# Projections with 128-row operands, the second feed-forward layer of two blocks by seven products, and a new instruction order

## The chip, the cores and the metric

One Trainium2 chip; the program runs on one of its NeuronCores. Five engines work side by side: PE (matrix multiply, with its weight loads listed as PEld), DVE (vector), ACT (activation), POOL (GpSimd) and SP, which here only issues DMAs. The metric is the device time of one execution in microseconds (us), the median over repeated executions.

## The reference

For 8 batches x 8 heads, 576 tokens, head size 64 and 128 random features, a linear attention is computed, and its output (4608 tokens x 512) goes through two dense layers of width 2048.

```python
def phi(x):                                  # x scaled by 64 ** -0.25
    proj = einsum('bhsd,md->bhsm', x, omega) # 64 -> 128
    h = proj - sum(x * x, -1) / 2
    return exp(h - max(h, -1)) / sqrt(m)
kv, z = einsum('bhsm,bhsd->bhmd', k_p, v), sum(k_p, 2)
num, den = einsum('bhsm,bhmd->bhsd', q_p, kv), einsum('bhsm,bhm->bhs', q_p, z) + 1e-6
h = x @ w_in                                 # x = num / den, 4608 x 512; w_in 512 x 2048
out = maximum(0.01 * h, h) @ w_out           # w_out 2048 x 512
```

All of it is float32; `q` is drawn 4.679 times as wide as `k` and `v`.

## The kernel before, in words

**Numbers in two halves.** A float32 operand of a matmul is scaled by a power of two and split into two float16 halves, high and low. A product takes three matmuls: high x high, high x low, low x high. Every split is an instruction on ACT or DVE that rounds (`high`, L331 on ACT) and one on DVE or POOL that subtracts (`low_`, L337).

**Feed-forward.** The 4608 tokens are 9 blocks of 512 (`feed_forward(j)`, j = 0 to 8). The first layer of blocks 0 and 1 is done plainly (L967). From block 2 on (`FIRST_FAST`) it is done by Strassen's method in Winograd's form: both matrices are cut into 2 x 2 quarters and 7 products of quarters take the place of 8 (`fast_first_layer`, L1007). The 2048 features are cut into four quads `q`; each quad has 7 products of 12 matmuls with 256 columns, whose weights come from a DRAM copy `w1d`. The intermediate results are copied out of PSUM (`so_far`, L331), added (`add`, L1023), passed through the leaky ReLU (L1030) and split into halves in the four tiles `big`. The second layer of every block is plain: four groups of 128 tokens, 48 matmuls of 512 columns each (`down`, L1084), 192 per block, one scaled copy out of PSUM and one store per group.

**Attention.** `Unit` prepares 512 (or 640) tokens of one pair of heads: load, squares and their sums, a scale, the two halves of the scaled tokens side by side in `z` (L539 to L562), and a transposing DMA `t<-z`. `project` (L578) then multiplies by omega. The two heads of a pair lie in the upper and the lower 64 rows, so every matmul uses 64 rows and there are three for each head and tile of 128 tokens: 24 for a unit of four tiles, 6 for the extra fifth tile of a key unit. Key batches 0 and 1 and query block 0 take another form in float32 (`Whole`, L645). Features then go through maximum, exponential and splitting; the sums over keys are at L773 to L775, the query products at L852 to L854.

**Order.** The kernel records all operations with a cost per engine and the tiles that they read and write; `Plan.order` then lays out one list of instructions per engine from these costs, priorities (`prio`), paces (`PACE`, `LATER`) and slacks (`SLACK`). Feed-forward matmuls are fillers: they go where PE has nothing more urgent. At run time each engine works its list strictly in that order.

**Start.** Before the feed-forward can run, w_in must be read as int64 words and rebuilt (L453 to L476), its scale found (sums over PE at L466, L486) and split (L500); and query block 0 must have passed through attention, up to the division at L872, the halves `xn` and the transposing DMA `xt<-xn`.

Of the kernel before, what the change touches and what calls it, by code (L numbers as in the profile page):

```python
# [30 lines left out]
SIGN_POOL = {"w1": [0, 1, 3, 4, 5, 7], "w2": [0, 1, 3, 7]}  # L31
SPLIT_DVE = {"w1": [0, 1, 2, 4, 5, 7], "w2": [0, 1, 2, 3, 4, 5]}
Z_POOL = {"k": 4, "q": 3}
PACE = {"k": 17.0506, "q": 9.805, "w1": 0, "w1s": 3.6719, "w2": 15.9561, "w2s": 15.0}

WHOLE = 2
FIRST_FAST = 2
OPS = ("A11", "A12", "A22", "S1", "S2", "S3", "S4")
SLOT = {"B11": 0, "B21": 1, "B22": 2, "B12": 3, "T1": 4, "T3": 5, "T2": 6, "T4": 7}
SLACK = {"PE": 0.5, "chain": 0.093}  # L40
SUMS_DVE = []
LATER = {"w1": -37.7982, "w2": 35.2434, "k": -22.3577, "q": -876.3298, "f": 0.0319, "s": -0.056}
# [5 lines left out]
OUT_UP = 2.0 ** 15 * 2.0 ** (-14 * 3)  # L48
# [19 lines left out]
class Plan:  # L68
# [7 lines left out]
    def __init__(self, places):  # L76
        self.places, self.ops, self.over = places, [], {}
        self.wrote, self.read, self.kinds = {}, {}, {}
        self.now, self.nth = (None, 0.0), 0
# [10 lines left out]
    def op(self, ways, r=(), w=(), prio=0.0, slack=0.0, moved=0):  # L90
# [4 lines left out]
        o.ways, o.prio, o.slack, o.moved = {e: way for e, *way in ways}, prio, slack, moved  # L95
        name, pace, self.nth = self.now[0], self.now[1], self.nth + 1
# [20 lines left out]
    def order(self):  # L117
# [51 lines left out]
        while len(done) < len(self.ops):  # L169
# [4 lines left out]
            for o in sorted(open_, key=lambda o: (o.prio, o.number)):  # L174
# [3 lines left out]
                if filler:  # L178
                    t += SLACK["PE"] * o.slack
# [24 lines left out]
            end = t + o.cost  # L204
# [3 lines left out]
            if e == "SP":  # L208
                ports = max(ports, end) + o.moved / 400e3
                end = ports + 1.9  # L210
            else:
                end += self.HOP[e]
# [43 lines left out]
def performer_ffn(ctx: ExitStack, tc, qT, kT, qn, kn, vn, omT, eye, w_in, w_out, out):  # L256
# [53 lines left out]
    for i in (6, 7):  # L310
        over["xt", len(tiles["xt"])] = [("w1", i)]
        tiles["xt"].append(tiles["w1"][i].bitcast(F16).rearrange("p (i c d) -> p i c d", i=2, c=8))
    plan = Plan({k: len(v) for k, v in tiles.items()})
# [49 lines left out]
    def power_of_two(mx, name, prio, one_=ONE):  # L363
# [6 lines left out]
           r=[f"mx_{name}", "ident"], w=["scratch"], prio=prio, slack=1.0)  # L370
# [46 lines left out]
    class Weight:  # L417
# [26 lines left out]
        def convert(self, i, prio):  # L444
# [17 lines left out]
            def sums():  # L462
# [6 lines left out]
               slack=6.0)  # L469
# [9 lines left out]
        def scale(self, prio):  # L479
# [11 lines left out]
            self.pow, self.key = power_of_two(mx, self.name, prio, ONE / 4 if self.name == "w1" else ONE)  # L491
# [28 lines left out]
    class Unit:  # L520


        def __init__(self, what, i, hp, prio):
            self.what, self.i, self.hp, self.prio = what, i, hp, prio
            tiles_ = key_tiles(i) if what == "k" else range(4 * i, 4 * i + 4)
            self.t0, self.nt = tiles_[0] * P, len(tiles_)

        def prepare(self):
# [15 lines left out]
            def scales():  # L544
# [6 lines left out]
                nc.vector.tensor_scalar(sc[:, 3:4], sc[:, 1:2], om_c, None, op0=ALU.mult)  # L551
            op("DVE", 0.65, scales, r=[self.sq, "om_c"], w=[self.sc], prio=prio)
            heads = lambda: at(nat)[:, :nt, :]
            up = lambda: at(self.sc)[:, 2:3]
            zh, zl = (lambda i=i: at(z)[:, :2 * nt, :].rearrange("p (c i) x -> p c i x", i=2)[:, :, i] for i in range(2))
# [11 lines left out]
        def features(self, c0, nc_, ph, part):  # L567
# [13 lines left out]
            op("PE", 3 * nc_ * 0.057, project, r=[self.t, "om"], w=[pj], prio=prio, slack=1.0)  # L581
# [6 lines left out]

            def bias():
                nc.vector.scalar_tensor_tensor(rows(1), rows(0), down(), sq(), op0=ALU.mult, op1=ALU.subtract)  # L590
# [3 lines left out]
            op("DVE", dve(n * M), lambda: nc.vector.scalar_tensor_tensor(p(), pv(), down(),  # L594
               row(2).rearrange("p (g o) -> p g o", o=1).broadcast_to([P, n, M]), op0=ALU.mult, op1=ALU.add),
               r=[pj, st, self.sc], w=[p32], prio=prio)
            op("ACT", act(n * M, 1), lambda: nc.scalar.activation(flat(p()), flat(p()), AF.Exp, bias=shift), w=[p32],  # L597
               r=["ones"], prio=prio)
# [12 lines left out]
    class Whole:  # L611
# [21 lines left out]
        def features(self, c0, nt, p32, p):  # L633
# [5 lines left out]
            def project():  # L639
# [9 lines left out]
               slack=1.0)  # L649
# [82 lines left out]
    def key_batch(b, prio):  # L732

        values(b, prio)
# [4 lines left out]
        for hp in range(HP):  # L739
            plan.like("k", PACE["k"])  # L740
            if b >= WHOLE:
# [12 lines left out]
            if b < WHOLE:  # L754
                def sums(u=u, edge=edge, acc=acc, hp=hp, parts=parts):
# [7 lines left out]
                   slack=1.0)  # L763
            else:
                def sums(u=u, edge=edge, acc=acc, hp=hp, parts=parts):
# [11 lines left out]
                   *((v, x) for x in (0, 1, 2, 3)), (v, "ones", 0), (v, "ones", 1)], w=[acc], prio=prio, slack=1.0)  # L777
# [19 lines left out]
    def parted(j, xn, xt, at_, n, src, keys, prio):  # L797
# [5 lines left out]
        low_(n * P, lambda: part(1), x, lambda: part(0), r=[*keys, (xn, 0)], engines=("POOL", "DVE"), w=[(xn, 1)],  # L803
             prio=prio)
# [3 lines left out]
    def query_block(j, prio):  # L808

        for hp in range(HP):  # L810
            plan.like("q", PACE["q"])
            u = Unit("q", j, hp, prio) if j else Whole("q", j, hp, prio)
# [25 lines left out]
            for i in range(2):  # L838
# [22 lines left out]
                if j:  # L861
                    op("PE", 12 * 0.031, num, r=[(qp, 0), (qp, 1), *((kvs[b], hp | 1) for b in used)], w=[acc],
                       prio=prio, slack=1.0)
# [48 lines left out]
    def fast_weights():  # L912
# [8 lines left out]
        for u in range(4):  # L921
            for k in range(2):
                b, b2 = buf("wt"), buf("wt")
                t = lambda i, b=b: at(b)[:, 256 * i:256 * i + 256]
# [22 lines left out]

    def feed_forward(j):
        plan.like()
        top, work = -1.0, 1e6 + j  # L950
        gs = [buf("big") for _ in range(4)]
        fast = j >= FIRST_FAST
# [28 lines left out]

        def fast_first_layer():
# [8 lines left out]
            def four_tiles(q):  # L991
                pair = lambda b: at(b).rearrange("p (f t) -> p f t", f=2)
# [186 lines left out]
```

## Time and profile before

| | us |
|---|---|
| median of 3 runs | 962.62 (961.75 to 963.24) |
| the profiled execution | 963.96 |
| its span, first to last instruction | 962.2 |
| PE busy in the span | 903.2 (94%) |
| DVE, ACT, POOL busy | 668.5, 574.1, 349.2 |
[...]

The profile shows one execution. Busy time of an engine is the time in which at least one of its instructions ran. In the timeline's rows of PE the duration of a group includes the run-out of its last matmul, so two groups that follow each other overlap on paper; the distance from one start to the next is what a group costs.

### The profile page before, as it was taken

What the parts mean: (1) busy time and instruction counts of PE and PEld (TensorE: products, weight loads), DVE (VectorE), ACT (ScalarE), POOL (GpSimd) and SP (SyncE); (2) the same over time, 40 slices, a digit from 0 to 9 for tenths busy, and PEclk for the clock granted to TensorE, in tenths of its full rate; (3) what the DMA queues carried; (4) which work ended last, traced back from release to release, by engine and by line L of the source; (5) the groups of instructions that cost most, each with busy time, mean ns of one, the idle gap of its engine ahead of it and who ended that gap; (6) DMA issues with size and microseconds to landing.
All of it is one profiled execution on the core that took longest, in us unless ns stands there. A gap on an engine that the chain in (4) does not pass through costs nothing.

```text
span 962.2 us, 20553 instructions
## 1 busy us (share of the span) xinstructions
PE 903.2 (94%) x8286; PEld 596.3 (62%) x8286; DVE 668.5 (69%) x1236; ACT 574.1 (60%) x833; POOL 349.2 (36%) x318
## 2 busy tenths in 40 slices
PE   4886999999998889999999999999999999999998
PEld 4785466445454775578557855785587558746843
DVE  7988998787689598878888787768788862200200
ACT  5686796647756676468746854686477634603520
POOL 2323346566755661116212621251125223400510
PEclk7778899999999999999999999999999999999999
DMA  9687335957398999799879878997689785623300
GB/s 369 264 238 244 67 56 116 223 155 176 59 195 210 296 277 209 166 238 239 185 179 234 203 195 184 221 238 158 140 217 236 149 149 160 172 57 102 96 12 33
DMA packets 278080, 171.19 MB, mean 178 GB/s; under 512 B 195296, under 2 KB 240096, under 8 KB 276960
## 3 DMA queue, kind: packets, MB, share of 16 engines
q1 hardware_dynamic: 277984, 169.87, 71.7%
q8 instruction: 65, 1.06, 0.5%
q14 instruction: 31, 0.25, 0.1%
HBM read 105.87 MB, written 16.78 MB: 127 GB/s over the span
## 4 chain that ended last, share of the span: by engine, by line
PE 70%; DVE 7%; DMA 7%; ACT 3%; issue 1%; SPq 1%; POOL 0%; ACTq 0%; DVEq 0%
PE ffn L1084 20%; PE ffn L1007 12%; PE pj L1084 11%; PE pj L1007 10%; PE ffn L967 7%; PE pj L578 4%; DMA qp<-ph 3%; DMA t<-z 2%; DMA w<-w1d 1%; PE pj L967 1%; DVE p L594 1%; ACT row L331 1%; DVE ph L337 1%; PE mi L852 1%; DVE st L586 1%
## 5 line engine op out<-in xcount | busy, mean ns | idle before, releaser
L337 POOL TENSOR_TENSOR big<-row,big 128x512 f16<-128x512 f32 x144 | 181.0, 1271 | 306.0 <-ACT big L331 284.0
L1084 PEld LDWEIGHTS <-big 128*128 128x128 f16 x1728 | 163.3, 98 | 183.8 <-issue 0.8
L1007 PEld LDWEIGHTS <-w 128*128 128x128 f16 x2352 | 227.1, 98 | 43.2 <-issue 8.7
L1084 PE MATMUL ffn<-wt,big 128*128 128x512 f16 x1056 | 246.4, 379 | 0.0
L1084 PE MATMUL pj<-wt,big 128*128 128x512 f16 x672 | 159.7, 379 | 0.6 <-ACT row L331 0.4
L1007 PE MATMUL ffn<-xt,w 128*128 128x256 f16 x1008 | 136.5, 273 | 2.4 <-DMA w<-w1d 1.7
L597 ACT ACTIVATE p<-p,little 128x1024 f32<-128x1024 f32 x68 | 70.1, 1031 | 70.4 <-DVE p L594 70.2
L1007 PE MATMUL pj<-xt,w 128*128 128x256 f16 x696 | 96.1, 273 | 3.7 <-ACT row L331 2.7
L586 DVE TENSOR_REDUCE st<-pj 128x8 f32<-128x1024 f32 x68 | 73.2, 1076 | 29.6 <-PE pj L578 29.4
L331 ACT ACTIVATE big<-row 128x512 f16<-128x512 f32 x144 | 87.2, 623 | 1.3
L1023 DVE TENSOR_TENSOR row<-ffn,row 128x512 f32<-128x512 f32 x47 | 32.1, 687 | 76.8 <-PE ffn L1007 48.3
L337 DVE TENSOR_TENSOR ph<-p,ph 128x1024 f16<-128x1024 f32 x56 | 70.4, 1257 | 11.6 <-ACT ph L331 11.6
L967 PE MATMUL ffn<-xt,w 128*128 128x512 f16 x312 | 73.2, 386 | 5.4 <-DMA xt<-xn 5.4
L594 DVE SCALAR_TENSOR_TENSOR p<-pj,sc,st 128x1024 f32<-128x1024 f32 x68 | 77.1, 1133 | 0.5
L967 PEld LDWEIGHTS <-w 128*128 128x128 f16 x384 | 36.5, 99 | 48.1 <-issue 7.9
L1030 ACT ACTIVATE row<-row 128x512 f32<-128x512 f32 x84 | 52.1, 622 | 20.9 <-DVE row L1023 20.9
L1007 PE MATMUL ffn<-w,w 128*128 128x256 f16 x372 | 60.9, 273 | 0.0
L331 ACT ACTIVATE ph<-p 128x1024 f16<-128x1024 f32 x56 | 58.9, 1053 | 1.0
L578 PE MATMUL pj<-om,t 64*128 64x128 f16 x1416 | 51.4, 217 | 6.9 <-DVE p L594 2.9
L578 PEld LDWEIGHTS <-t 64*128 64x128 f16 x1416 | 40.1, 94 | 26.9 <-issue 24.0
L539 ACT ACTIVATE z<-nat 128x512 f32<-128x512 f32 (+1 forms) x56 | 36.3, 648 | 33.7 <-DMA t<-z 28.5
L337 POOL TENSOR_TENSOR v<-xp,v 128x768 f16<-128x768 f32 (+1 forms) x15 | 25.2, 1681 | 83.3 <-ACT v L331 79.0
(126 smaller groups left out, 1520.6 us busy)
## 6 DMA issues: line engine op xcount, KB each, us to landing
w<-w1d SPq DMA_DIRECT2D x196, 256.0 KB, 3.5
v<-vn SPq DMA_DIRECT2D x28, 650.0 KB, 4.7
out<-row SPq DMA_DIRECT2D x36, 256.0 KB, 2.5
big<-w_in SPq DMA_DIRECT2D x8, 1024.0 KB, 10.2
big<-w_out SPq DMA_DIRECT2D x8, 1024.0 KB, 5.6
nat<-qn SPq DMA_DIRECT2D x32, 256.0 KB, 3.4
w1d<-wt SPq DMA_DIRECT2D x16, 256.0 KB, 2.8
nat<-kn SPq DMA_DIRECT2D x12, 320.0 KB, 3.5
```

The costliest lines, as they stand in the source:

```text
L331: ("ACT", act(n, int(pointer)), lambda: nc.scalar.activation(dst(), src(), AF.Copy, scale=1.0 if scale is None else value()), False),
L337: return ways([(e, c, lambda g=g: g.tensor_tensor(dst(), a(), b(), op=ALU.subtract), True) for e, c, g in (("POOL", pool_(n), nc.gpsimd), ...
L539: op("ACT", act(n), lambda: nc.scalar.activation(square(), flat(at(nat)[:, :nt, :]), AF.Square, scale=SQ_SCALE), r=[nat], w=[z], prio=prio)
L578: nc.tensor.matmul(at(pj)[:, 512 * h + c * M:512 * h + (c + 1) * M], at(self.t)[r, 2 * (c0 + c) + zp, :], om[r, op_, :], start=(zp == op_ ...
L586: op("DVE", dve(n * M), lambda: nc.vector.tensor_reduce(row(0), pv(), axis=AX.X, op=ALU.max), r=[pj], w=[st], prio=prio)
L594: op("DVE", dve(n * M), lambda: nc.vector.scalar_tensor_tensor(p(), pv(), down(), row(2).rearrange("p (g o) -> p g o", o=1).broadcast_to([ ...
L597: op("ACT", act(n * M, 1), lambda: nc.scalar.activation(flat(p()), flat(p()), AF.Exp, bias=shift), w=[p32], r=["ones"], prio=prio)
L967: nc.tensor.matmul(at(ph), wk[wp][:, c:c + P], xt[:, 512 * xp:512 * xp + 512], start=(i == 0), stop=(i == 3 * KT - 1))
L1007: nc.tensor.matmul(pair(bank)[:, f], wt[:, k, wp, f * P:f * P + P], operand(xname, k, xp), start=(first and f == k == i == 0), stop=(k == ...
L1023: op("DVE", dve(512), lambda: nc.vector.tensor_tensor(at(u), at(bank), at(u), op=ALU.add), r=[bank], w=[u], prio=top)
L1030: op("ACT", act(512), lambda: nc.scalar.activation(at(g), at(src), AF.Prelu, scale=H_DOWN, alpha=0.01), r=[src], w=[g], prio=top)
L1084: nc.tensor.matmul(at(po), g_(q)[:, s, gp, t * P:(t + 1) * P], wf[wp], start=(q == s == 0 and gp == wp), stop=(q == s == 3 and gp == 1))
```

## The change

1. **Projections.** In `z` the halves are now laid out head by head, high half in 64 columns and low half in the next 64, so that after the transposing DMA one head fills all 128 rows. The matmul with `om[:, 0]` (omega's high half, standing in both halves of the rows) and the one with `om[:, 1]` (its low half) give four terms, low x low too. A unit has 16 matmuls of 128 rows in place of 24 of 64 rows, the fifth tile 4 in place of 6.
2. **Second layer of blocks 7 and 8** (`TAIL = 7`): seven products in place of eight. The sums of quarters of w_out are built once (`tail_weights`: 32 additions and 16 splits of 128x512). The first layer of these blocks yields seven operands per quad and not four: four additions (`combine`) and seven splits. They lie in 28 places of 512 columns: 16 in `big` and 12 in tiles that attention no longer uses. The second layer then has 7 x 4 groups of 12 matmuls with 256 columns, 336 per block, and its results are scaled and added on ACT and DVE (`so_far`, `add`).
3. **Order and small settings.** New paces, slacks and a table `NUDGE` that shifts priorities of single units; costs of DVE and POOL in the planner scaled (`SLOWER`). `Z_POOL` rises from 4 to 6 for keys and 3 to 7 for queries, so 24 more units scale their tokens in place on ACT before splitting. One of eight sets of w_in sums goes from POOL to DVE (`SUMS_DVE = [2]`). The scale of w_out's split is `ONE / 4`.

```diff
-Z_POOL = {"k": 4, "q": 3}
+Z_POOL = {"k": 6, "q": 7}
+TAIL = 7
+TAIL_ON = {"A11": ["DVE"], "A22": ["DVE"], "S1": ["DVE"], "S3": ["DVE"], "S2": ["POOL"], "A12": ["DVE"], "S4": ["DVE"], "T1": ["POOL"], "T2": ["DVE"], "T3": ["DVE"], "T4": ["DVE"]}
+NUDGE = {"k00": -7.29, "w24": 1.48, "q61": -17.43, "k10": 0.44, "k51": 15.04, "q00": -3.82, "k53": 5.68, "w20": 3.7, "w2s6": 16.56, "k12": -4.82, "w1s0": 20.35, "q41": 14.5, "w1s4": -32.18, "w2s5": 11.73, "q72": -10.0, "q03": -2.3, "w1s7": 13.37, "w2s7": 35.19, "k61": -6.36, "w13": -2.71, "w2s3": -4.27, "q10": 5.76, "s1": -0.42, "k50": -35.27, "q70": 36.43, "q02": 2.72, "q40": 2.15, "k42": 7.0, "w25": 5.84, "q63": -12.37, "w27": 3.08, "k11": 0.9, "w26": 10.91, "w2s2": -8.29}
+SLOWER = {"ACT": 1.0, "DVE": 1.041, "POOL": 0.95, "PE": 1.0, "SP": 1.0}
-SUMS_DVE = []
+SUMS_DVE = [2]
...
+    for k, n in (("row", ROWS_LATE), ("tt", 16), ("g7", 12)):
+        for _ in range(n):
+            host, place_ = spare.pop(0)
+            over[k, len(tiles[k])] = [host]
+            tiles[k].append(place_)
...
-            zh, zl = (lambda i=i: at(z)[:, :2 * nt, :].rearrange("p (c i) x -> p c i x", i=2)[:, :, i] for i in range(2))
+            zh, zl = lambda: at(z)[:, :2 * nt, :D], lambda: at(z)[:, :2 * nt, D:]
...
                 for c in range(nc_):
-                    for zp, op_ in ((0, 0), (0, 1), (1, 0)):
-                        for h in range(2):
-                            r = slice(64 * h, 64 * h + 64)
+                    for h in range(2):
+                        for w in range(2):
                             nc.tensor.matmul(at(pj)[:, 512 * h + c * M:512 * h + (c + 1) * M],
-                                             at(self.t)[r, 2 * (c0 + c) + zp, :], om[r, op_, :],
-                                             start=(zp == op_ == 0), stop=(zp == 1))
+                                             at(self.t)[:, 2 * (c0 + c) + h, :], om[:, w, :], start=(w == 0),
+                                             stop=(w == 1))
...
+            for dst, x, y, sign in ((2, ("B12", 0), ("B12", 1), ALU.add), (0, ("B11", 0), ("B11", 1), ALU.add),
+                                    (0, 2, 0, ALU.subtract), (1, ("B22", 0), ("B22", 1), ALU.add),
+                                    (2, 1, 2, ALU.subtract), (1, 1, 0, ALU.subtract),
+                                    (3, ("B21", 0), ("B21", 1), ALU.add), (3, 3, 1, ALU.subtract)):
...
+                op("DVE", stt(512), lambda sums=sums: sums(nc.vector), port=True, r=r, w=[key(dst)], prio=LATER["t"])
+            for name, i in (("T3", 2), ("T2", 1), ("T1", 0), ("T4", 3)):
+                tt = tts[name, q] = buf("tt")
...
+                    if tail:
+                        have[half, t] = g
+                        if not t:
+                            split("A12" if half else "A11", q, g)
+                            if half:
+                                combine(g, g, have[0, 0], ALU.subtract)
+                                split("S4", q, g)
+                        elif half:
+                            split("A22", q, g)
+                        else:
+                            combine(have[1, 1], g, have[1, 1], ALU.add)
+                            split("S1", q, have[1, 1])
+                            combine(g, have[0, 0], g, ALU.subtract)
+                            split("S3", q, g)
+                            combine(have[0, 0], have[1, 1], have[0, 0], ALU.subtract)
+                            split("S2", q, have[0, 0])
+                        return
...
+            a = buf("ffn")
+            product(a, "A11", "B11", True, False)
+            u1 = so_far(a, 0)
+            c = buf("ffn")
+            product(c, "S3", "T3", True, False)
+            product(a, "S2", "T2", False, False)
+            u2 = so_far(a, 1)
+            d = buf("ffn")
+            product(d, "A12", "B21", True, True)
+            add(u1, d, 0)
+            store(u1, 0, 0)
+            product(a, "S1", "T1", False, True)
+            u3, u4 = so_far(a, 1), so_far(a, 0)
+            add(u3, c, 1)
+            store(u3, 1, 1)
+            b = buf("ffn")
+            product(b, "S4", "B22", True, True)
+            add(u4, b, 0)
+            store(u4, 0, 1)
+            product(c, "A22", "T4", False, True)
+            add(u2, c, 1)
+            store(u2, 1, 0)
```

The order moves at two places of interest. The first is DVE near the end of the start, between the fifth and the eighth of the divisions of query block 0 (`xp<-mi,r`); `wt` and `w` are pieces of the weights. Before:

```order
L872 TENSOR_TENSOR xp_106<-mi_134,r_125 128x256
L458 SCALAR_TENSOR_TENSOR wt_73<-big_81,wt_73 128x1024
L500 SCALAR_TENSOR_TENSOR w_4_65<-wt_77,little,w_4_65 128x1024
L500 SCALAR_TENSOR_TENSOR w_5_66<-wt_70,little,w_5_66 128x1024
L869 TENSOR_SCALAR r_126<-mi_134 128x4
L870 RECIPROCAL r_126<-r_126 128x4
L872 TENSOR_TENSOR xp_106<-mi_134,r_126 128x256
```

The same place of the changed kernel, where line numbers are some 30 to 50 higher:

```order
L919 TENSOR_TENSOR xp_106<-mi_134,r_125 128x256
L487 SCALAR_TENSOR_TENSOR wt_73<-big_80,wt_73 128x1024
L529 SCALAR_TENSOR_TENSOR w_4_65<-wt_77,little,w_4_65 128x1024
L916 TENSOR_SCALAR r_126<-mi_134 128x4
L917 RECIPROCAL r_126<-r_126 128x4
L366 TENSOR_TENSOR w_3_64<-wt_75,w_3_64 128x1024
L919 TENSOR_TENSOR xp_106<-mi_134,r_126 128x256
```

Two subtractions of 1024 columns for w_in still stand ahead of the sixth division, but one of them is now the split of another piece, and the whole list up to the eighth division is one such subtraction shorter (116 instructions, 117 before).

The second place is DVE in the last block's first layer. Before, DVE has only the additions out of PSUM there (two of the four tiles `row` and a PSUM bank in each):

```order
L1023 TENSOR_TENSOR row_3_105<-ffn_1_132,row_3_105 128x512
L1023 TENSOR_TENSOR row_0_102<-ffn_0_131,row_0_102 128x512
L1023 TENSOR_TENSOR row_1_103<-ffn_2_133,row_1_103 128x512
L1023 TENSOR_TENSOR row_3_105<-pj0_0_130,row_3_105 128x512
L1023 TENSOR_TENSOR row_2_104<-ffn_2_133,row_2_104 128x512
```

In the changed kernel the additions out of PSUM (L1118) stand between the sums of operands (L1074) and their splits (L366), in the tiles that attention has left (`nat`, `z`, `v`, `xn`, `xp`):

```order
L1118 TENSOR_TENSOR nat_1_84<-ffn_2_133,nat_1_84 128x512
L1074 TENSOR_TENSOR nat_0_83<-row_1_103,nat_0_83 128x512
L366 TENSOR_TENSOR big_0_79<-z_0_85,big_0_79 128x512
L1074 TENSOR_TENSOR row_1_103<-z_0_85,row_1_103 128x512
L366 TENSOR_TENSOR v_0_98<-nat_0_83,v_0_98 128x512
L1118 TENSOR_TENSOR row_3_105<-ffn_0_131,row_3_105 128x512
L366 TENSOR_TENSOR xn_0_107<-nat_1_84,xn_0_107 128x512
L366 TENSOR_TENSOR xn_0_107<-row_3_105,xn_0_107 128x512
```

Per quad there are 3 additions out of PSUM, 4 sums and 6 splits on DVE, 13 in all in place of 3; the splits of S2 alone stay on POOL.

## Rows read from the trace of the kernel before

**Rows 1.** The page's head, busy time of PE and DVE, PE's 40 slices and clock.
```profile
span 962.2 us, 20553 instructions
PE 903.2 (94%) x8286; PEld 596.3 (62%) x8286; DVE 668.5 (69%) x1236; ACT 574.1 (60%) x833; POOL 349.2 (36%) x318
PE   4886999999998889999999999999999999999998
PEclk7778899999999999999999999999999999999999
```

**Rows 2.** Stretches of the span: length, busy us per engine, clock, DMA share, GB/s.
```profile
0.00:98.00 98.00, 68.41 (x646) 61.82 (x647) 81.73 (x123) 65.08 (x77) 28.33 (x22) 0.77 0.82 276
98.00:300.00 202.00, 198.78 (x1654) 105.89 (x1654) 172.01 (x305) 137.22 (x193) 119.12 (x118) 0.99 0.63 134
300.00:360.00 60.00, 49.82 (x584) 40.04 (x583) 48.75 (x88) 40.53 (x63) 35.11 (x35) 1.00 1.04 274
360.00:796.00 436.00, 426.27 (x4326) 283.77 (x4325) 346.92 (x694) 274.22 (x402) 126.37 (x111) 1.00 0.85 197
796.00:962.20 166.20, 159.93 (x1082) 104.76 (x1079) 19.11 (x30) 57.01 (x99) 40.30 (x34) 1.00 0.32 90
```

**Rows 3.** Waits of PE in the first 98 us: total, times, longest.
```profile
PE ffn L466 <- DVE wt L458: 9.5, 3, 4.2
PE ffn L967 <- DMA xt<-xn: 5.4, 1, 5.4
PE mi L859 <- DVE xp L872: 4.2, 1, 4.2
```

**Rows 4.** The chain that ended last, two pieces of the tail: start, us, matmuls.
```profile
803.11 5.24 PE ffn L1007 x48
...
839.74 15.54 PE ffn L1084 x72
```

**Rows 5.** Timeline of PE around one projection unit and one fifth tile.
```profile
501.70 1.46 PE L1084 MATMUL ffn<-wt,big 128*128 128x512 f16 x6
503.10 0.84 PE L578 MATMUL pj<-om,t 64*128 64x128 f16 x24
503.87 1.47 PE L1084 MATMUL pj<-wt,big 128*128 128x512 f16 x6
...
199.33 0.34 PE L578 MATMUL pj<-om,t 64*128 64x128 f16 x6
199.61 1.68 PE L1084 MATMUL ffn<-wt,big 128*128 128x512 f16 x7
```

**Rows 6.** Weight loads at the same place, and their idle time over the span.
```profile
503.09 0.67 PEld L578 LDWEIGHTS <-t 64*128 64x128 f16 x24 [0.42 <-issue]
504.96 0.53 PEld L1007 LDWEIGHTS <-w 128*128 128x128 f16 x4
...
PEld L578 <- issue: 24.0, 58, 2.3
```

**Rows 7.** PE's query products, each with 128x128 weights of its own, and these loads.
```profile
508.67 0.19 PE L854 MATMUL mi<-kv,qp 128*128 128x65 f16 x1
508.85 0.19 PE L854 MATMUL mi<-kv,qp 128*128 128x65 f16 x1
...
L852 PEld LDWEIGHTS <-qp 128*128 128x128 f16 (+1 forms) x288 | 24.3, 99 | 9.8 <-issue 2.5 <-DMA qp<-ph 1.6
```

**Rows 8.** DVE and ACT, 128x512: groups back to back, and one form's mean.
```profile
246.25 0.69 DVE L887 TENSOR_TENSOR xp<-xp 128x512 f32<-128x512 f32 x1
246.85 0.69 DVE L337 TENSOR_TENSOR z<-nat,z 128x512 f16<-128x512 f32 x1
...
886.74 1.40 DVE L1023 TENSOR_TENSOR row<-ffn,row 128x512 f32<-128x512 f32 x2 [5.99 <-ACT row L331]
...
889.76 1.14 ACT L331 ACTIVATE big<-row 128x512 f16<-128x512 f32 x2
...
L887 DVE TENSOR_TENSOR xp<-xp 128x512 f32<-128x512 f32 x14 | 13.8, 984 | 0.1
```

**Rows 9.** DVE around the sixth division, and the end of the kernel.
```profile
78.06 4.57 DVE L500 SCALAR_TENSOR_TENSOR w<-wt,little,w 128x1024 f16<-128x1024 f32 x2
74.60 1.22 DVE L337 TENSOR_TENSOR w<-wt,w 128x1024 f16<-128x1024 f32 x1
...
954.05 4.05 PE L1084 MATMUL pj<-wt,big 128*128 128x512 f16 x18
958.20 0.69 ACT L331 ACTIVATE row<-pj,s 128x512 f32<-128x512 f32 x1 [3.20 <-PE pj L1084]
```

More of the change, by code (lines that the diff above doesn't have):

```diff
@@ L203, in order @@
             o.cost, o.run, held = o.ways[e]
-            end = t + o.cost
+            end = t + o.cost * SLOWER[e]
             free[e] = end
@@ L208, in order @@
             if e == "SP":
-                ports = max(ports, end) + o.moved / 400e3
-                end = ports + 1.9
+                ports = max(ports, end) + o.moved / 400e3 * (DMA["turn"] if o.cost > 1.0 else 1.0)
+                end = ports + DMA["land"]
             else:
@@ L312, in performer_ffn @@
         tiles["xt"].append(tiles["w1"][i].bitcast(F16).rearrange("p (i c d) -> p i c d", i=2, c=8))
+    spare = []
+    for k, n in (("nat", 1), ("z", 1), ("t", 1), ("kv", 1), ("p32", 2), ("ph", 2), ("qp", 2), ("xp", 4), ("vr", 2),
+                 ("v", 5), ("xn", 2)):
+        for i in range(len(tiles[k])):
+            whole_tile = tiles[k][i]
+            names = " ".join("abcd"[:len(whole_tile.shape) - 1])
+            whole_tile = whole_tile.rearrange(f"p {names} -> p ({names})") if " " in names else whole_tile
+            whole_tile = whole_tile.bitcast(F32) if k in ("z", "t", "ph", "qp", "xn") else whole_tile
+            spare += [((k, i), whole_tile[:, 512 * n_:512 * n_ + 512]) for n_ in range(n)]
+    tiles["g7"], tiles["tt"] = [], []
+    for i in range(16):
+        over["g7", i] = [("big", i // 4)]
+        tiles["g7"].append(tiles["big"][i // 4][:, 512 * (i % 4):512 * (i % 4) + 512])
+    for k, n in (("row", ROWS_LATE), ("tt", 16), ("g7", 12)):
[3 more added lines that the diff above has]
+            tiles[k].append(place_)
     plan = Plan({k: len(v) for k, v in tiles.items()})
@@ L732, in key_batch @@
     def key_batch(b, prio):
+        plan.group = f"v{b}"
         values(b, prio)
@@ L948, in feed_forward @@
     def feed_forward(j):
         plan.like()
+        plan.group = None
         top, work = -1.0, 1e6 + j
-        gs = [buf("big") for _ in range(4)]
-        fast = j >= FIRST_FAST
+        fast, tail = j >= FIRST_FAST, j >= TAIL
+        gs = [buf("big") for _ in range(4)] if not tail else None
+        g7 = {}
         g_ = lambda q: at(gs[q]).bitcast(F16).rearrange("p (f i t) -> p f i t", f=4, i=2)
@@ L1074, in feed_forward @@
         batches = {(512 * j + x) // S for x in (0, 511)}
-        op("DVE", 0.2, lambda: nc.vector.tensor_scalar(at(s4), row_scale[:, 4 * j:4 * j + 4], wexp, None,
-           op0=ALU.mult), r=["wexp", *(f"rows{b}" for b in batches)], w=[s4], prio=top)
+        op("DVE", 0.2, lambda: nc.vector.tensor_scalar(at(s4), row_scale[:, 4 * j:4 * j + 4], wexp,
+           1.0 / TAIL_DOWN if tail else 1.0, op0=ALU.mult, op1=ALU.mult), r=["wexp", *(f"rows{b}" for b in batches)],
+           w=[s4], prio=top)
@@ L1077, in feed_forward @@
+        if tail:
+            fast_second_layer()
+            return
         for t in range(4):
```

163 lines of the change are left out of this document (137 added, 26 removed).

## The prediction

> **What bounds the kernel now.** I read the page's busy times first: PE works 903.2 of 962.2 us, no other engine more than 668.5, and the slices of PE are full but for the first four and a few in the middle [rows 1]. Then the stretches (length, then busy PE, PEld, DVE, ACT, POOL): PE idles 29.6 us before 98.0, when the feed-forward begins to run without a break, then 3.2, 10.2 (at a DMA share of 1.04) and 9.7 us, and 6.3 us after 796, where only the feed-forward is left [rows 2]. Of the last, 4.1 us lie behind the last matmul, which ends at 954.05 + 4.05 = 958.10 [rows 9]. The clock is 0.77 before 98 and at its upper level from there on. So the kernel is a start whose length DVE sets (81.7 of 98 us busy) and then a PE that hardly waits: a matmul column taken from PE after 98 us shortens the run, and work added to other engines costs only where PE comes to wait for it.
>
> **The change part by part.** The sum is made against the profiled execution, 963.96 us (1.8 beyond its span, 1.3 above the median of 962.62).
>
> *Second layer of blocks 7 and 8.* Before, 192 matmuls of 512 columns at 15.54 / 72 = 0.2158 us: 41.4 us a block. After, 336 of 256 columns at 5.24 / 48 = 0.1092 us (the first layer's products have this shape): 36.7 us [rows 4]. That is 4.76 us a block, all of it in a stretch where PE has 159.9 of 166.2 us of work [rows 2]: -9.5 us.
>
> *Projections.* The count of a unit goes from 24 to 16, but its 24 matmuls go in pairs on the two halves of the array: from 503.10 to 503.87 they cost 0.77 us, 0.032 each. To that comes 0.10 us before them: the group at 501.70 should end at 501.70 + 6 x 0.2158 = 503.00 [rows 5]. The weight loads explain it: those of the 64-row matmuls begin at 503.09, after 0.42 us idle for which the profile names nothing, and there are 58 such pauses, while a load of 128 rows starts at 504.96, ahead of the group at 505.18 that it serves [rows 6]. So a unit costs 0.87 us now. After, 16 matmuls of 128 columns with 128 rows. No row has this shape; a half of 0.1092 is 0.055, and the other end is a load that nothing hides, 0.099 [rows 7]. I take 0.055, since loads of the same size follow each other every 0.030 us at the query products (508.67 to 508.85, six starts [rows 7]), and no pause: 0.87 us, no difference over 56 units. The 12 fifth tiles go from 0.28 + 0.10 [rows 5] to 4 x 0.055 = 0.22: -1.9 us. If the pause stays, 68 x 0.10 = +6.8 us comes back.
>
> [...]
>
> *Work for the tail's other engines.* A quad of the first layer of blocks 7 and 8 is 7 groups of 1.31 us on PE, 9.17 us. DVE gets 13 instructions of 128x512 for it: 0.60 us apart when independent (246.25 to 246.85), 0.70 when not (1.40 for two) [rows 8], so 7.8 to 9.1 us. ACT gets 3 copies, 4 activations and 7 roundings at 1.14 / 2 = 0.57 [rows 8]: 8.0 us. Both fit, with little to spare. In block 7 come 4 x 8 sums and 12 splits for w_out's quarters, 44 x 0.65 = 29 us more for DVE. In the new order 62 DVE instructions stand between the last query block's last operand and the last split of T3 (37 to 43 us), and PE has 42 groups (55 us) ahead of the product that needs it. So I book +2 us of small waits, with ends 0 and, by the form whose mean is 0.98 [rows 8], 8 quads x (13 x 0.98 - 9.17) = +29. All single rows of that size in rows 8 are near 0.7, so the low end is near.
>
> *End.* One copy of 0.69 us behind the last matmul [rows 9] becomes two additions of 256 columns, some 0.8 by half of 0.70 each and a start; the store has as many bytes: +0.1.
>
> *Start.* One DVE instruction of 1.22 us [rows 9] fewer ahead of the last division of query block 0: -1.2 us, if DVE is what that waits for, as its 4.2 us before the sixth division say [rows 3] (the two splits at 78.06 took 4.57 us [rows 9]). The largest single wait there is 5.4 us for `xt<-xn` [rows 3], so -5.4 to +5.4.
>
> *Rest of the order.* 24 more units scale their tokens on ACT, 24 x 0.6 = 14 us, hidden as ACT is busy 315 of the 496 us from 300 to 796 [rows 2]; uncovered, it would stand ahead of `t<-z` once a unit. Eight sums of 256 columns leave POOL for DVE, about 0.4 each by half of 0.69 and a start, in stretches where DVE has room. What the new order does to the 23 us of idle PE between 98 and 796 [rows 2] can't be read off rows: 0, with ends -5 and +5.
>
> Sum: -9.5 - 1.9 + 2 + 0.1 - 1.2 = -10.5 us, so 953.5 in the profiled execution, and 952.1 against the median.
>
> **The rivals.**
> *Weights not hidden (slower).* If a 128-row matmul of the projection must wait for its own load, it takes 0.099 us [rows 7] and a unit 1.58: +0.71 x 56 and nearly nothing at the fifth tiles, +40, so 992. It turns the sign from 0.065 us a matmul on (10.5 / 896 = 0.012 above 0.055). Against it: starts 0.030 us apart where every matmul has such a load [rows 7]. [...] Chance 0.05.
> *The tail waits for DVE.* At 0.80 us an instruction, a third of the way from 0.70 to that mean of 0.98, a quad takes 10.4 us and not 9.17, 8 quads 10 us more in place of my 2: 960. For it: the fit is tight and DVE goes in a fixed order. Against it: DVE has 19 us of work in this stretch now [rows 2], and the second layer's groups, which need little of DVE, stand between. Chance 0.14.
> *The new order gives more.* If it takes a further third of the 29.6 us idle at the start or of the 23 in the middle: 944. For it: the waits in rows 3 are of a kind that order alone decides. Against it: DVE was busy 81.7 of 98 us there. Chance 0.23.
> *The new order takes back.* Projections of 0.97 us (pause kept, +6.8) and 4 us lost in the middle leave 963. Chance 0.11.
> *The forecast*, 948 to 957: 0.47.
>
> **How the numbers follow.** The likeliest is 952. The range 942 to 964 leaves out the unhidden weights, the worst of the tail and the best of the order. Two executions of this kernel differ by about 0.2%, 1.9 us, so that is what a measurement can tell from no change. Faster takes the forecast, the third rival and most of the second: 0.80. Same, 0.09, and slower, 0.11, share the order that takes back, the unhidden weights and the worst of the tail.
>
> **What would show it.** In the changed profile: groups of 12 matmuls of the second layer at 1.31 us; a projection unit 0.87 to 0.90 us from its start to the next, without the pause before its weight loads, and about 0.22 for a fifth tile; PE idle after the last query product within some 4 us of before (2.2 us apart from the end); the feed-forward's unbroken run beginning at 93 to 98 us. Wrong it is if the projections' starts are more than 0.065 us apart, if PE's waits in the last 150 us for DVE or ACT exceed 8 us, or if the first unbroken run begins after 101 us.

## The result and the profile after

The changed kernel took 939.03 us (937.94 to 941.42, 4 runs) where the kernel before took 962.93 in the same comparison: ratio 0.9756, 95% interval 0.9733 to 0.9778. That is 23.9 us less, where 10.5 were forecast; 939.0 also lies below the range of 942 to 964. On another chip the same kernel came to a ratio of 0.9797 (0.9772 to 0.9821, run e5), so its gain is 20 to 24 us.

The page's head, and stretches of the same stages as in [rows 1, 2] (length, then busy PE, PEld, DVE, ACT, POOL, clock, DMA share, GB/s):

```profile
span 936.7 us, 20382 instructions
PE 886.2 (95%) x8102; PEld 633.8 (68%) x8102; DVE 752.0 (80%) x1384; ACT 606.9 (65%) x905; POOL 326.5 (35%) x290
PE   4786999999999799999999999999999999998998
PEclk7897999999999999999999999999999999999999
```

```profile
0.00:90.80 90.80, 60.76 (x645) 53.98 (x646) 79.54 (x124) 64.38 (x77) 29.84 (x22) 0.83 0.89 298
90.80:300.00 209.20, 205.50 (x1561) 113.72 (x1561) 179.68 (x321) 141.56 (x200) 125.22 (x123) 0.99 0.63 147
300.00:360.00 60.00, 54.63 (x596) 45.60 (x595) 46.07 (x90) 43.44 (x71) 25.14 (x24) 0.97 0.90 235
360.00:775.00 415.00, 411.55 (x3903) 285.97 (x3902) 340.60 (x688) 279.65 (x415) 126.39 (x110) 1.00 0.86 201
775.00:936.70 161.70, 153.80 (x1403) 134.54 (x1401) 106.08 (x165) 77.88 (x143) 19.87 (x14) 1.00 0.35 98
```

The start is 7.1 us shorter (90.8 for 97.9), although PE idles as long in it: 30.0 us for 29.6. What differs is its clock, 0.83 for 0.77. From there to the tail PE idles 3.7 + 5.4 + 3.5 = 12.6 us, where it was 3.2 + 10.2 + 9.7 = 23.1 [rows 2]. The tail idles 7.9 us for 6.3, with DVE at 106 us of work for 19.

The timeline of PE around a projection unit, a fifth tile, two groups of the new second layer, and the end, for [rows 4, 5, 9]:

```profile
508.39 1.06 PE L609 MATMUL pj<-om,t 128*128 128x128 f16 x16
509.28 0.19 PE L899 MATMUL mi<-kv,qp 128*128 128x65 f16 x1
...
197.33 0.39 PE L609 MATMUL pj<-om,t 128*128 128x128 f16 x4
197.56 1.46 PE L1284 MATMUL ffn<-wt,big 128*128 128x512 f16 x6
...
916.27 1.47 PE L1209 MATMUL pj<-ph,big 128*128 128x256 f16 x12
917.58 1.47 PE L1209 MATMUL ffn<-wt,big 128*128 128x256 f16 x12
...
931.06 1.47 PE L1209 MATMUL ffn<-xp,big 128*128 128x256 f16 x12
```

From start to start: 0.89 us for the unit (0.0556 a matmul), 0.23 for the fifth tile, 1.31 for a group of 12. A pause of the kind in [rows 6] is nearly gone: PEld of L609 has 2.3 us of it in 2 times, where L578 had 24.0 in 58.

### The profile page after: what moved, and what is told of

The parts are those of the page before. It is cut to its first block, busy times and chain, and to the rows that moved or that the text cites. A ratio compares the mean times of both kernels' runs of the same rounds, so it can differ in the third digit from the quotient of the medians.

```text
span 936.7 us, 20382 instructions
## 1 busy us (share of the span) xinstructions
PE 886.2 (95%) x8102; PEld 633.8 (68%) x8102; DVE 752.0 (80%) x1384; ACT 606.9 (65%) x905; POOL 326.5 (35%) x290
## 4 chain that ended last, share of the span: by engine, by line
PE 82%; DVE 8%; DMA 4%; ACT 3%; issue 2%; SPq 1%; DVEq 0%; ACTq 0%
PE ffn L1284 16%; PE ffn L1102 14%; PE pj L1284 12%; PE pj L1102 10%; PE ffn L1048 6%; PE pj L609 5%; PE ffn L1209 5%; PE pj L1209 3%; PE pj L688 2%; PE pj L1048 2%; DMA xt<-xn 1%; DMA t<-z 1%; PE mi L899 1%; DVE wt L487 1%; PE mi L806 1%
## 5 line engine op out<-in xcount | busy, mean ns | idle before, releaser
L366 POOL TENSOR_TENSOR big<-row,big 128x512 f16<-128x512 f32 x116 | 148.5, 1292 | 272.5 <-ACT big L360 261.8
L1284 PEld LDWEIGHTS <-big 128*128 128x128 f16 x1344 | 127.3, 98 | 136.3
L1284 PE MATMUL ffn<-wt,big 128*128 128x512 f16 x816 | 190.2, 379 | 0.0
L1102 PE MATMUL ffn<-xt,w 128*128 128x256 f16 x1044 | 140.8, 274 | 3.3 <-DMA xt<-xn 3.1
L1284 PE MATMUL pj<-wt,big 128*128 128x512 f16 x528 | 124.1, 379 | 0.0
L360 ACT ACTIVATE big<-row 128x512 f16<-128x512 f32 x128 | 77.1, 621 | 3.0 <-DVE row L1074 2.3
L366 DVE TENSOR_TENSOR ph<-p,ph 128x1024 f16<-128x1024 f32 x56 | 72.6, 1296 | 6.8 <-ACT ph L360 6.6
L609 PE MATMUL pj<-om,t 128*128 128x128 f16 x944 | 64.0, 219 | 4.2 <-DMA t<-z 2.4
L609 PEld LDWEIGHTS <-t 128*128 128x128 f16 x944 | 57.7, 98 | 14.6 <-DMA t<-z 3.7
L366 POOL TENSOR_TENSOR v<-xp,v 128x768 f16<-128x768 f32 (+1 forms) x15 | 26.5, 1768 | 86.5 <-ACT v L360 86.4
L571 DVE TENSOR_REDUCE sq<-z 128x8 f32<-128x512 f32 (+1 forms) x56 | 39.6, 708 | 18.5 <-ACT z L569 18.4
L1125 ACT ACTIVATE row<-row 128x512 f32<-128x512 f32 x71 | 43.8, 623 | 14.2 <-DVE row L1118 13.8
```

Of the source, the lines that this page charges most:

```text
L360: ("ACT", act(n, int(pointer)), lambda: nc.scalar.activation(dst(), src(), AF.Copy, scale=1.0 if scale is None else value()), False),
L366: return ways([(e, c, lambda g=g: g.tensor_tensor(dst(), a(), b(), op=ALU.subtract), True) for e, c, g in (("POOL", pool_(n), nc.gpsimd), ...
L571: op("DVE", dve(n), lambda: nc.vector.tensor_reduce(at(self.sq)[:, :2 * nt], square().rearrange("p (g d) -> p g d", d=D), axis=AX.X, op=AL ...
L1102: nc.tensor.matmul(pair(bank)[:, f], wt[:, k, wp, f * P:f * P + P], operand(xname, k, xp), start=(first and f == k == i == 0), stop=(k == ...
L1125: op("ACT", act(512), lambda: nc.scalar.activation(at(g), at(src), AF.Prelu, scale=H_DOWN * (TAIL_DOWN if tail else 1.0), alpha=0.01), r=[ ...
L1284: nc.tensor.matmul(at(po), g_(q)[:, s, gp, t * P:(t + 1) * P], wf[wp], start=(q == s == 0 and gp == wp), stop=(q == s == 3 and gp == 1))
```

## The experiments

Ratios are to the kernel before, run on the same chip beside each. There are eighteen runs, e1 to e18; unless the text says otherwise, a time is a median. Lines marked `...` stand for code left out.

**The parts and the order, taken apart**

*e1, the projections alone, in the old kernel.*

```diff
-                    for zp, op_ in ((0, 0), (0, 1), (1, 0)):
-                        for h in range(2):
...
+                    for h in range(2):
+                        for w in range(2):
...
```

> The kernel before with the projections of 128 rows and four terms as its only edit; every engine keeps its order. Theory A (the 13 us that I did not forecast come from the order that the new settings make): only the projections' own sum, 56 units x +0.02 us (0.89 for 0.87) and 12 fifth tiles x -0.15, about -0.7, so 961 to 963. Theory B (the parts themselves are worth more than their instructions show, because the pauses at the old projections also held up their neighbours): 10 to 13 us less, 950 to 953.

Measured 965.07, ratio 1.0012 (0.9991 to 1.0034): no difference that can be told, as theory A has it.

*e2, both parts under the old settings.*

```diff
-Z_POOL = {"k": 6, "q": 7}
+Z_POOL = {"k": 4, "q": 3}
-SLOWER = {"ACT": 1.0, "DVE": 1.041, "POOL": 0.95, "PE": 1.0, "SP": 1.0}
+SLOWER = {"ACT": 1.0, "DVE": 1.0, "POOL": 1.0, "PE": 1.0, "SP": 1.0}
+NUDGE = {}
...
-            op("PE", 4 * nc_ * 0.056, project, r=[self.t, "om"], w=[pj], prio=prio, slack=SLACK["t"])
+            op("PE", 3 * nc_ * 0.057, project, r=[self.t, "om"], w=[pj], prio=prio, slack=SLACK["t"])
```

`SLACK`, `PACE`, `LATER`, `SIGN_POOL` and `SUMS_DVE` go back to their values of before as well.

> The changed kernel with all of the planner's settings (NUDGE, SLACK, SLOWER, PACE, LATER, SIGN_POOL, Z_POOL, SUMS_DVE and the projection's price) put back to those of before: projections and seven products without the new order. Theory A: what my sum gave for the two parts, -9.5 -0.7 and 0 to +2 for the tail's work on the other engines, 952 to 955, with the start as before (unbroken feed-forward run from about 98 us) and 10 us of idle TensorE in 300 to 360. Theory B: near the changed kernel, 939 to 943. A third (theory C, the tail's new work needs the new order): above 958, with TensorE idle for DVE in the last 160 us.

Measured 961.95, ratio 0.9986 (0.9954 to 1.0017): theory C by its time. Two parts that save some 10 us of matmuls bring 1.4 (from 4.4 less to 1.6 more). The stretches (busy PE alone, then clock, DMA share, GB/s), first of before in the same division, then of e2, cut at the run's start, 300 us, the last query product and the last matmul:

```profile
0.00:97.92 97.92, 68.33 (x646) 0.77 0.82 277
97.92:300.00 202.08, 198.86 (x1654) 0.99 0.63 134
300.00:797.91 497.91, 478.01 (x4934) 1.00 0.87 205
797.91:958.10 160.19, 158.01 (x1056) 1.00 0.32 92
```

```profile
300.00:803.91 503.91, 483.66 (x4604) 0.99 0.86 203
803.91:957.67 153.76, 146.83 (x1326) 1.00 0.33 94
```

The tail takes 6.4 us less and not 9.5, with PE idle for 6.9 us in it (2.2 before); 5.0 of them are waits for ACT and 2.0 for DVE, where theory C had DVE. And it begins 6.0 us later. That is not more waiting: from 300 us to the last query product PE idles 20.3 us for 19.9, and is busy 5.7 us longer. A lower clock can have a part in that: in e2's profile it was 0.66 from 311.8 to 316.8 us, with 31 matmuls there and 56 in the 5 us behind, and 0.66 from 561.8 to 566.8, with 29 and then 51. How much is work that the new plan does ahead of the tail stays open.

*e3, the settings alone (old projections, no seven products in any second layer), and e4, the changed kernel with the old projections.*

```diff
-TAIL = 7
+TAIL = 9
...
-                    for h in range(2):
-                        for w in range(2):
...
+                    for zp, op_ in ((0, 0), (0, 1), (1, 0)):
+                        for h in range(2):
...
```

The first two lines are e3's alone; the rest is in both.

> The changed kernel with the old projections and with TAIL = 9, so no block has seven products: the settings alone. Theory A: the whole of the unexplained gain, 963 less 12 to 15, so 948 to 951, with the unbroken run from about 91 us and 10 us less idle TensorE after it. Theory B: 961 to 964. Theory C (the settings pay only together with the parts): 957 to 961.

> The changed kernel with the 24 products of 64 rows back in place of the 16 of 128; the order of all engines stays that of the changed kernel. Theory A: 0.7 more than 939, so 939 to 941, with a pause of about 0.1 us back at each unit. Theory B: 949 to 952.

e3: 952.87, 0.9900 (0.9865 to 0.9934). e4: 948.29, 0.9862 (0.9821 to 0.9903). The settings alone bring 10 us: theory A, 2 us short of its size. e4 lies just under theory B's 949 to 952, far from A; e5 was run to see whether that is the chip.

*e5, the changed kernel again, and e6, it without the seven products (`TAIL = 9`).*

> The changed kernel unaltered, on the chip of this call. The two kernels with the old projections and with the parts in the old order were timed on a chip whose runs spread by 9 us, so the 9 us between the changed kernel (939.0) and the same with the old projections (948.3) may be that chip's. If the difference is the projections': 938 to 941. If it is the chip's: 944 to 948, with the query products' milestones as late as there (last one about 792 us).

> The changed kernel with TAIL = 9: new settings and new projections, plain second layer in all blocks. Theory A (parts by their sums, the rest by the order): 9.5 less 1.6 of more tail waits over the changed kernel, 946 to 949 where that is 939, and 0.7 under the settings alone (952.9). If the projections are worth the 9 us that the old ones seemed to cost in the new order: 943 to 945, 9 under the settings alone.

e5: 943.72, 0.9797 (0.9772 to 0.9821). e6: 955.26, 0.9926 (0.9901 to 0.9950). e5 comes out just under the branch that has the chip as the reason, and e6 lies above both of its branches. Now e4 and the changed kernel have the same order on every engine, and so have e3 and e6. Each pair sets the old projections against the new ones, with the layout of `z` that goes with each, and nothing else, as e1 does. With the new ones the time is 1.7 us more in e1, 2.4 more in e6 against e3, and 4.6 less in e5 against e4 (by the ratios +1.2, +2.5 and -6.3, with 2 to 5 us of uncertainty in each). The forecast of about -0.7 lies among them; what makes them differ in sign isn't shown.

**The start**

e6 and the changed kernel have the same instructions in the same order on PE up to about 300 us, and e6's profiled execution (962.98) is one in which the start was slow: its unbroken run begins at 96.59 us, not 90.80. The stretch before, first of the changed kernel, then of e6:

```profile
50.00:53.00 3.00, 1.81 (x23) 1.00 0.40 66
53.00:61.00 8.00, 7.90 (x78) 0.79 0.82 264
61.00:69.00 8.00, 7.16 (x76) 1.00 1.14 252
```

```profile
50.00:53.00 3.00, 1.81 (x23) 0.98 0.43 101
53.00:61.00 8.00, 8.00 (x63) 0.50 0.73 241
61.00:69.00 8.00, 8.00 (x54) 0.50 0.86 246
```

In both the clock falls at 53 us, behind PE's two waits of 1.6 and 1.2 us: from 53 to 56 us it is 0.51 in the one and 0.50 in the other. In the one it is back after some 3 us (0.94 from 56 to 60), in the other it stays at 0.50 up to 69 us at least, for 16. In the kernel before the clock was 0.51 from 57 to 67.5 us. That suggested a test: matmuls that compute nothing in the start's planned waits.

*e9, these in the changed kernel, and e10, in the kernel before.*

```diff
-        for o in plan.order():
...
+        for o in planned:
+            if o.engine == "PE":
+                if 4.0 < o.start < until and o.start - last > 0.5:
+                    for _ in range(int((o.start - last) * 0.8 / 0.06)):
+                        nc.tensor.matmul(at(wsums)[:, 256:376], ident.bitcast(BF16)[:, :P],
+                                         ident.bitcast(BF16)[:, P:P + 120], start=True, stop=True)
+                last = o.start + o.cost
             o.run()
```

> The changed kernel with 421 matmuls that compute nothing (128x120, on the identity matrix, into 120 unused columns of a PSUM bank) put into the start's planned waits of TensorE; every other instruction stands as before. In profiles of one and the same start the unbroken feed-forward run began at 90.8, 91.1 and 96.6 us: with the granted clock at 1.00, 1.00 and 0.50 from 61 to 67 us. If the clock's falls after the start's waits set its length: clock over 0.9 from 20 to 80 us, run from 86 to 90 us, and 3 to 6 us less than the changed kernel (ratio to the kernel before 0.970 to 0.976, where that was 0.976 and 0.980). If the start hangs on the transfers and VectorE instead: run from 90 us on, ratio 0.978 to 0.983.

> The kernel before with 451 such matmuls in its planned waits of the start, all else as it was. If the 7 us that the changed kernel's start is shorter are the clock's (0.63 granted from 60 to 70 us before, 1.00 after): the unbroken run begins 4 to 8 us earlier than 97.9 and the ratio is 0.992 to 0.996. If they are the new order's own: begins at 96 to 98, ratio 0.998 to 1.002.

e10: 956.81, 0.9928 (0.9907 to 0.9949). The kernel before gains 7.8 us by 451 matmuls of no use. Its stretches, and its plain first-layer rows:

```profile
0.00:90.72 90.72, 77.70 (x1096) 1.00 0.89 299
90.72:300.00 209.28, 205.63 (x1738) 1.00 0.61 138
300.00:790.64 490.64, 471.19 (x4850) 1.00 0.88 205
790.64:950.84 160.20, 158.02 (x1056) 1.00 0.31 92
```

```profile
87.34 0.81 PE L967 MATMUL ffn<-xt,w 128*128 128x512 f16 x3
90.72 2.10 PE L967 MATMUL ffn<-xt,w 128*128 128x512 f16 x9 [2.58 <-DMA xt<-xn]
```

The clock is 1.00 from the first us on, the run begins at 90.72 and not 97.92, and from there to the last matmul everything is as long as before: 860.1 us for 860.2. DVE, ACT and POOL have the same instructions in the same order as before.

e9: 942.96, 0.9788 (0.9758 to 0.9819), its second branch: no faster than e5, with the clock at 1.00 and the run at 90.44, behind a wait of 4.3 us for `xt<-xn` that more clock does not take away:

```profile
0.00:90.44 90.44, 76.39 (x1066) 1.00 0.88 300
```

```profile
90.44 1.86 PE L1048 MATMUL ffn<-xt,w 128*128 128x512 f16 x4 [4.29 <-DMA xt<-xn]
```

So the shorter start is worth 7 to 8 us, and the clock alone gives it to the old order. At a clock of 1.00 the two orders' starts are equally long (90.72 and 90.44 us). The new order comes near that floor without help in six of the seven profiles that share its start (90.8 to 92.9; 96.6 in e6). Why its waits leave the clock higher isn't shown.

**What the seven products cost beside the matmuls**

*e12, e2 with plain quarters of w_out in place of the sums T1 to T4.*

```diff
+            plain = {"T1": "B11", "T2": "B12", "T3": "B21", "T4": "B22"}
...
+                name = plain.get(name, name)
...
-            tail_weights()
```

> The projections and the seven products under the old settings, as in e2 (962, where the parts' sum gave 952 to 955), but the four sums of w_out's quarters, T1 to T4, are left out, and a plain quarter stands in the place of each, so the output isn't the reference's: VectorE is spared some 50 us in the middle. If preparing the sums beside the middle's blocks is what ate the parts' gain: 951 to 955, ratio 0.986 to 0.991, the last query product before 799 us. If it is the tail's own waits or the order as such: 959 to 963, ratio 0.995 to 1.0.

954.51, 0.9907 (0.9876 to 0.9938): 7.4 us under e2, as the first branch has it. The tail idles 2.9 us for 6.9:

```profile
300.00:798.03 498.03, 479.51 (x4575) 0.99 0.87 204
798.03:949.50 151.47, 148.57 (x1345) 1.00 0.34 97
```

But DVE is spared only 28 us (731.8 for 759.7), and the plan is made anew; since plans differ by several us of their own (below), how much of the 7.4 is the sums' own stays open.

*e13, e2 with the fillers of e10.*

> The kernel of e2 (projections and seven products under the old settings) with the 451 matmuls that compute nothing in the start's planned waits. They took 7.8 us off the kernel before. If the start's clock and the parts add up: 953 to 956, ratio 0.988 to 0.992; what then still lies between it and the changed kernel (ratio 0.976 to 0.980), 9 to 12 us, is the middle's and the tail's waits. If the clock's gain is eaten by later waits: 960 to 963.

955.12, 0.9908 (0.9885 to 0.9931). The clock's 7 to 8 us and the parts' 1.4 add up. From here to the changed kernel are 11 to 15 us. The work is the same but for what the settings move between engines (`Z_POOL`, `SUMS_DVE`) and the matmuls of no use; the rest of the difference is the order.

**Which setting carries the rest**

*e7: `NUDGE = {}`. e8: `SLOWER` all 1.0. e11: `NUDGE` with the 11 shifts of k0, k1, q0 and w1 alone. e14: `Z_POOL = {"k": 4, "q": 3}`. Each is the only edit to the changed kernel.*

> The changed kernel with NUDGE empty, so that no unit of work is moved ahead of or behind its turn; all else stays. If the 34 single shifts carry the new order's gain (12 to 14 us): 949 to 953, with the waits of query products for qp<-ph back in 300 to 400 us (6 of them, 6.4 us, before). If the settings that hold for whole groups carry it: 939 to 943.

> The changed kernel with SLOWER at 1.0 for all engines, so the planner reckons VectorE 4 per cent faster and GpSimd 5 per cent slower than the changed kernel's does; the plan is thereby made anew from the start. If the gain hangs on prices that fit the chip: 945 to 952. If any new order with these weights does as well: 938 to 942.

> The changed kernel with the 11 shifts of the start's groups (k0, k1, q0, w1) kept in NUDGE and the 23 of later ones left out; TensorE's order is that of the changed kernel up to its row 5643 (about 330 us). Leaving out all 34 cost 10 us. If that was in the middle (query products waiting again for qp<-ph, 7.4 us there): ratio 0.987 to 0.992, the last query product at 795 us or later, the start as in the changed kernel. If it was in the start: 0.978 to 0.982.

> The changed kernel with Z_POOL put back to k 4, q 3: in 24 units of keys and queries the lower half of z is made again by one VectorE instruction from PSUM-free inputs with the scale, where the changed kernel makes a scaled copy on ScalarE or VectorE first. If VectorE's relief in the middle carries the rest of the gain: ratio 0.988 to 0.994 and more of TensorE's waits for p, qp and t. If not: 0.976 to 0.983.

e7: 953.31, 0.9902 (0.9878 to 0.9925). e8: 959.46, 0.9963 (0.9948 to 0.9979). e14: 954.62, 0.9899 (0.9868 to 0.9930). Each of these three results, taken alone, seems to say that just this setting carries the gain; e8 lost even more than its branch had. e11: 944.34, 0.9806 (0.9772 to 0.9841): leaving out 23 of the 34 shifts does nothing that can be measured, although it makes another order (on DVE from about 105 us on, on PE from about 330).

*e15 and e16: e13 with the new `Z_POOL` and with the new price of a projection (`4 * nc_ * 0.056`).*

> The kernel of e13 with one setting more, Z_POOL at the new k 6, q 7. If VectorE's relief carries the rest: 4 to 10 us under e13, idle TensorE between the unbroken run and the last query product down from 28 to 20 us or less. If it has no part of its own: within 3 us of e13.

> The kernel of e13 with only the planner's price of a projection at what it takes (0.896 for a unit of 16 where the old plan reckons 0.684; 0.89 measured), so that the plan no longer runs 12 us ahead of TensorE by the end. If an honest price carries the rest (the plan counts on transfers that in truth land later): 4 to 10 us under e13. If not: within 3 us of it.

e15: 963.24, 1.0000 (0.9978 to 1.0021). e16: 960.75, 0.9966 (0.9950 to 0.9982). Both are 6 to 8 us slower than e13, outside both branches of either. In this order, neither DVE's relief nor an honest price brings a gain by itself.

*e17 and e18: the planner's landing time of a transfer 0.05 us longer, in the changed kernel and in the one before.*

```diff
-DMA = {"turn": 1.0, "land": 1.9}
+DMA = {"turn": 1.0, "land": 1.95}
...
-                end = ports + 1.9
+                end = ports + 1.95
```

The first pair of lines is e17's, the second e18's.

> The changed kernel with the planner's time from the end of a transfer's move to its use at 1.95 us in place of 1.9: no engine, no data and no instruction changes, only the order that comes out (TensorE's differs from its row 1021 on). If the gain that no single setting carries is one of a whole order that fits the chip, a neighbour in the settings loses it as the three others did (no shifts +9.6, equal prices +15.7, old Z_POOL +10.9): 947 to 957, ratio 0.983 to 0.993. If the new settings make good orders as such: 939 to 945, ratio 0.975 to 0.981.

> The kernel before with the same 0.05 us put on its planned landing time; its TensorE order differs from row 379 on. If every order that a planner makes untried falls about as far from a fitted one, and that of before was fitted in the same way: 970 to 980, ratio 1.007 to 1.017. If the order of before is one like any other: within 5 us of it on either side, 0.995 to 1.005.

e17: 956.27, 0.9925 (0.9894 to 0.9957). A number that changes no work costs 12.5 us against e5. e18: 968.04, 1.0027 (1.0001 to 1.0054): 0.3% on before. The stretches, first of the changed kernel, then of e17:

```profile
0.00:90.80 90.80, 60.76 (x645) 0.83 0.89 298
90.80:300.00 209.20, 205.50 (x1561) 0.99 0.63 147
300.00:785.11 485.11, 476.29 (x4592) 1.00 0.86 204
785.11:932.53 147.42, 143.69 (x1308) 1.00 0.34 96
```

```profile
0.00:90.82 90.82, 60.65 (x646) 0.83 0.89 298
90.82:300.00 209.18, 201.88 (x1525) 0.99 0.60 142
300.00:801.61 501.61, 484.02 (x4653) 1.00 0.87 201
801.61:949.08 147.47, 141.28 (x1284) 1.00 0.33 91
```

The starts are equal to 0.02 us, the tails as long. From the start's end to the last matmul PE idles 7.3 + 17.6 + 6.2 = 31.1 us for 3.7 + 8.8 + 3.7 = 16.2. That is spread over many small waits; between 300 and 770 us (total, times, longest), of before, of the changed kernel and of e17:

```profile
PE mi L854 <- DMA qp<-ph: 6.4, 6, 1.5
PE pj L578 <- DMA w<-w1d: 2.3, 1, 2.3
PE pj L578 <- DVE p L594: 2.0, 2, 1.4
PE pj L1007 <- ACT row L331: 1.8, 4, 0.7
```

```profile
PE ffn L1102 <- DMA xt<-xn: 3.1, 1, 3.1
PE pj L1102 <- ACT row L360: 2.7, 5, 0.7
PE mi L901 <- DMA qp<-ph: 2.2, 1, 2.2
PE pj L609 <- DMA t<-z: 0.5, 1, 0.5
PE ffn L1102 <- ACT row L360: 0.2, 1, 0.2
```

```profile
PE pj L1102 <- ACT row L360: 3.2, 4, 1.0
PE mi L901 <- DMA qp<-ph: 3.1, 3, 1.3
PE pj L1102 <- DVE row L1118: 3.0, 4, 1.4
PE ffn L1102 <- DMA xt<-xn: 2.3, 1, 2.3
```

The changed kernel's rows end there, with 8.7 us in all; the first four of before and of e17 alone sum to 12.5 and 11.6. Before, the query products' waits for `qp<-ph` led; in e17 DVE, ACT and transfers share. So what the changed kernel's order has is fewer waits, not one wait less. None of the versions tried beats it beyond the interval.

## Why the prediction was wrong

- *Second layer, -9.5: held as a count.* The groups of 12 take 1.31 us as forecast. As a time it depends on the settings around it: under the old ones both parts bring 1.4 us (e2), on top of the new ones some 10 (0.9900 in e3, 0.9797 in e5).
- *Projections, 0 over the units, -1.9 over the fifth tiles: held within what the runs can tell* (e1 +1.2, from -0.9 to +3.3; the other two pairs +2.5 and -6.3). A unit takes 0.89 us without the pause, a fifth tile 0.23. The rival of weights not hidden is out: a matmul takes 0.89 / 16 = 0.056 us, where that rival had 0.099 [rows 7].
- *Work for the tail's other engines, +2: held in the new order, not in the old.* Between the last query product and the last matmul PE idles 3.7 us for 2.2. In e2 it is 6.9, more for ACT (5.0) than for DVE (2.0), which my rival had named. Without the sums of w_out's quarters it is 2.9 (e12).
- *Start, -1.2 with an end at -5.4: the first step that failed.* It measured -7.1, and the run began at 90.8 us, ahead of the 93 to 98 that I gave. I had called it a start whose length DVE sets, and had looked for a wait or a DVE instruction that goes; but PE idles as long as before, and in e10 DVE's list is untouched and the run begins 7.2 us earlier. What goes is time at the lower clock, and e10 shows 7.8 us of it in the old order. [rows 2] had the number in plain sight, a clock of 0.77 over 98 us, and I put no price on it. With matmuls of no use in the start's waits it was 1.00 there, in e10 and in e9.
- *Rest of the order, 0 from -5 to +5: the second.* It measured -10.5 in the middle's idle PE, in place of 23.1 us 12.6. By e13 against the changed kernel it is worth 11 to 15 us in all, tail included. I had put it at nothing because rows could not tell it, and the ends of 5 us rested on no row; e7, e8, e14 and e17 show orders of nearly the same work 10 to 16 us behind the changed kernel's. The rival "the new order gives more" named the right thing; at 944 it gave the order a part of the start or of the middle, and both came.
- In sum, from the two profiles in the stretches of [rows 2]: the start -7.2, PE's work behind it -9.4 (834.8 us before, 825.4 after; forecast -11.4), its idle time in the middle -10.5, in the tail and behind it +1.6. That is -25.5, the whole of 962.2 to 936.7. So in this order PE's work and the tail came out within 2 us of the sum, and what goes beyond it are the two steps above, by 6.0 and 10.5 us.
- In sum, from the runs: start 7 to 8 (e10), parts 1.4 under the old settings (e2), the order 12.5 (e17 against e5). That makes 21 to 22, where 20 to 24 were measured. The runs allow another division as well: the settings alone some 10 (e3), the parts on top of them some 10 (e3 to e5, with 4 us of uncertainty). The shares depend on what is put in first, and none is the effect of one part by itself.
- Smaller slips: the 0.2% between two executions came from three runs; beside e17 the kernel before took 959.4 to 969.9, a spread of 1%. A third of the start's 29.6 us would have given 942 and not 944, and 0.065 us a matmul for the turn of the sign should be 0.067. Nothing hung on the last two.

Shown is that the last 12.5 us hang on the order: in e17 no instruction changes, and PE idles 14.9 us more behind an equal start. Four of the five settings tried beside the changed kernel's lose 10 to 16 us (e7, e8, e14, e17), so no one of them can be called the cause; the fifth (e11) makes another order too and loses nothing, so not every new order loses. Not shown is what makes the good orders better than their neighbours, beyond fewer waits, nor how this one was come by; only one neighbour of the order before was tried, and it lies 0.3% away.

## What to carry to other kernels

A change that makes a planned order anew is two changes: price the parts by their instructions, but give the order a range as wide as neighbouring plans differ (here 944 to 960 us for nearly the same work), and don't read a cause from one setting put back. Where a start runs at a low granted clock, price that clock as a term of its own, and try matmuls of no use in its waits before any rearranging; here that gave 7.8 us in one kernel and nothing in the other, whose start was already at the length that a clock of 1.00 gives. Work added to engines off the path has to be checked for every engine that hands PE its operands: in e2 the tail waited longer for ACT than for DVE.

## What was not expected of the hardware

- 451 matmuls of 128x120 on constant data, in planned waits of the first 90 us, made a kernel of 963 us faster by 7.8 us (0.9907 to 0.9949).
- The same instructions behind the same two waits stood at a clock of 0.51 for 3 us in one profile (the changed kernel) and of 0.50 for at least 16 in another (e6, which has the same start), and the run behind them began 5.8 us later.
- A lower clock comes in the middle too: in e7 it was 0.66 from 720 to 725 us; of the 5 us from 713.9 to 718.9 PE was busy for 3.6.
